# Issuing the mixer's streamed weights from SyncE's DMA queue instead of GpSimd's

## The chip, the core and the metric

The kernel runs on one core of a Trainium2 chip. The time is device microseconds of one execution; several executions give a median. All rows of a profile come from one profiled execution, which has a time of its own.

## What is computed

Four layers in a row on x of 2048 tokens by 640 numbers (bf16): attention with a recurrent memory (A), a mixer with an MLP (B), and both again with the same weights. Each layer is added to x after a layer norm.

```python
x = x + A(layernorm(x));  x = x + B(layernorm(x))
x = x + A(layernorm(x));  x = x + B(layernorm(x))

# A: 64 segments of 32 tokens, one after the other; 32 heads of 192
mem = mem0                                    # 8 x 640
for s in range(64):
    h = concat([mem, x[32*s:32*s+32]])        # 40 x 640
    q, k, v = h @ Wq, h @ Wk, h @ Wv          # 640 -> 32 x 192 each
    o = softmax(mask(q @ k.T * 192**-0.5)) @ v
    o = o @ Wo                                # 32 x 192 -> 640
    mem = o[:8];  out[s] = o[8:]

# B: c = 160, the four quarters of h moved by 1, -1, 2, -2 tokens
h  = gelu(layernorm(x) @ w1)                  # 640 -> 640
x1 = x + shift_quarters(h) @ w2               # 640 -> 640
y  = x1 + gelu(layernorm(x1) @ w3) @ w4       # 640 -> 1536 -> 640
```

## The kernel before

**Steps.** A segment needs the memory of the segment before it, so attention is a chain of 64 steps. The kernel runs both attention layers together: in step t, lane 0 is segment t of the first attention layer and lane 1 is segment t - 5 of the second (LAG = 5). There are 69 steps. The first five and the last five have one lane (40 columns in a matmul), the others two (80 columns). After each second step a chunk of the mixer (64 tokens of each lane, 128 rows) becomes ready; its work is spread among the matmuls of the steps that follow. There are 35 chunks.

**Weights.** Wq, Wk, Wv and Wo are cut into 8 groups of four heads. A group of Wq, Wk or Wv has five blocks of 128 rows by 768 columns (192 KB), a group of Wo has six of 128 by 640 (160 KB). They do not all fit in SBUF. By CUT, three blocks of each group of q, k and v and four of each group of o (two of the first) stay resident; the others are streamed from HBM anew in each step (block, lines 428 to 451, issued at line 447). The mixer's weights are streamed anew in each chunk: 5 blocks of w1, 5 of w2, 12 of w3 and 12 of w4, each 128 by 640 (load_b, lines 453 to 467, issued at line 465). The parts of w1, w3 and w2 that do not lie as a block in HBM are written once, at the start, in block order to a scratch tensor in HBM (wbd, order_mixer_weights, lines 469 to 490, from GpSimd's queue).

**The ring.** Streamed blocks of both kinds go into one ring of 16 slots (wst). Attention may hold at most 14 of them at a time (RING_A), the mixer at most 6 (RING_B). A slot comes free when TensorE has finished the matmuls on its block.

**The order.** Nothing is scheduled by the compiler. Every operation is added to a planner (Plan.add) with its engine, an estimated duration, a due time, and what it reads and writes. Plan.place (lines 134 to 246) plays the program through: at each turn it takes, of all engines, the operation that can start first, and among those of one engine that can start within 0.05 us (0.03 on TensorE) the one with the earliest due time. Streamed attention loads form the queue "wa" and mixer loads the queue "wb"; only the head of each is on offer. The order found is the order in which each engine's instructions are written; on the chip each engine runs its own list in that order and waits on semaphores.

Loads issued from SyncE (SP) obey one more rule: a load may start only when the tenth-last load of SP has landed, in the plan by est, and on the chip by a dependency that is written in at the end:

```python
def est(o, t):                                              # line 163
    s = max(t, o.ready)
    if o.dma and o.e == "SP" and len(landed) >= FLIGHT:     # FLIGHT = 10
        s = max(s, landed[-FLIGHT])
...
for o in placed:                                            # line 1094
    ins = o.fn(o)
    if o.dma and o.e == "SP":
        if len(flight) >= FLIGHT:
            tc.add_manual_dep(ins.ins, flight[-FLIGHT].ins.name, ...)
        flight.append(ins)
```

The mixer's loads are issued by one function, whose engine depends on a constant:

```python
def load_b(c, nm, n, due):                                  # line 453
    b = ring("rb")
...
    def fn(op):
        return (nc.sync if B_SP else nc.gpsimd).dma_start(out=T(b)[:, 0:Dm], in_=src)
    add("SP" if B_SP else "POOL", SP_US if B_SP else POOL_US, due, fn, r=rd, w=(b,),
        dma=P * Dm * 2, queue="wb")
```

**Other names.** TensorE's projections are at lines 530 (k and q) and 571 (v), the output projection at 669, scores, transposes and P V at 602, 635 and 650. The mixer's matmuls are at 939 (w1), 961 (w2), 993 (w3) and 1011 (w4). GpSimd also issues the loads and stores of activations (lines 823 to 834 and 1029) and computes the powers of the layer norms (741, 898).

Of the kernel before, what the change touches and what calls it, by code (L numbers as in the profile page):

```python
# [22 lines left out]
RING = 16  # L23
RING_A = 14
RING_B = 6
B_SP = False
POOL_US = 0.9
SP_US = 0.47
CUT = {"k": [3] * 8, "q": [3] * 8, "v": [3] * 8, "o": [2] + [4] * 7}
# [55 lines left out]
class Plan:  # L85
# [11 lines left out]
    def add(self, e, d, due, fn, r=(), w=(), a=(), dma=0, queue=None, after=()):  # L97
        op = Op()
        op.e, op.d, op.due, op.fn, op.dma = e, d, due, fn, dma
        op.succ, op.ready, op.n = [], 0.0, 0  # L100
        op.i = len(self.ops)
        preds = set(after)
        slots = []
        for b in r:
            preds.update(b.writers)
        for b in w:
            preds.update(b.writers)
            preds.update(b.readers)
        for b in a:
            preds.update(b.base)  # L110
            preds.update(b.readers)
        for b in r:
            b.readers.append(op)
        for b in w:
            b.base = [op]
            b.writers = [op]
            b.readers = []
        for b in a:
            b.writers.append(op)
        for b in {id(b): b for b in (*r, *w, *a)}.values():  # L120
            if isinstance(b, Slotted):
                b.left += 1
                slots.append(b)
        op.slots = slots
        preds.discard(op)
        for p in preds:
            p.succ.append(op)
            op.n += 1
        self.ops.append(op)
        if queue is not None:  # L130
            self.queues.setdefault(queue, []).append(op)
        return op
# [117 lines left out]
def kernel(  # L250
# [148 lines left out]
    def T(b):  # L399
        if b.obj is None:  # L400
            b.obj = b.make()
        return b.obj
# [50 lines left out]
    def load_b(c, nm, n, due):  # L453
# [10 lines left out]
        def fn(op):  # L464
            return (nc.sync if B_SP else nc.gpsimd).dma_start(out=T(b)[:, 0:Dm], in_=src)  # L465
        add("SP" if B_SP else "POOL", SP_US if B_SP else POOL_US, due, fn, r=rd, w=(b,), dma=P * Dm * 2, queue="wb")
        return b, lambda: T(b)[:, 0:Dm]
# [669 lines left out]
```

## Time and profile before

| | |
|---|---|
| median of 3 runs | 3576.57 us (3575.23 to 3577.35) |
| the profiled execution | 3575.23 us |
| its span, first to last instruction | 3573.5 us |
| mean granted TensorE clock | 0.989 |
| weight transfers from SP (line 447) | 4554, of 192 or 160 KB |
| weight transfers from GpSimd (line 465) | 1190, of 160 KB |
| bytes moved, mean rate | 1097.76 MB, 307 GB/s |

How to read it: PE is TensorE's matmuls and PEld its weight loads, DVE is VectorE, ACT ScalarE, POOL GpSimd, SP SyncE, and SPq the queue of instructions on SP, all of which issue or wait. A busy share is an average over the span. A row of waits names the engine and line that waited, after the arrow what ended the wait (an engine's instruction or a DMA's landing), and then the total in us, the number of times and the longest. "DMA share" is how much of the time the 16 DMA engines were moving packets, on average. Queue q1 carries what SP issues, q0 what POOL issues. A transfer of 128 rows is split among the 16 DMA engines; it has landed when all 16 are done.

### The profile page before, as it was taken

The page shows a single profiled execution, that of the slowest core. Times are in us where ns is not written, and L with a number is a line of the kernel's source. Part 1 is how long each engine was busy: PE and PEld are TensorE (multiplying, and loading weights), DVE is VectorE, ACT ScalarE, POOL GpSimd, SP SyncE. Part 2 cuts the span into 40 slices and gives each one's busy share as a digit, 9 for nine tenths or more (in the row PEclk, how much of TensorE's full clock was granted, in tenths as well). Part 3 has the DMA queues.
Part 4 walks back from the last instruction along what each step waited for, and adds up shares of the span by engine and source line. Part 5 has one row for each costly group of instructions (what it writes and reads, how often), then busy time and mean ns, then how long its engine had stood idle before and what let it go on. Part 6 is the DMA issues. An engine that isn't in the chain of part 4 may idle for free.

```text
span 3573.5 us, 194593 instructions
## 1 busy us (share of the span) xinstructions
PE 3398.9 (95%) x84703; PEld 3260.5 (91%) x84703; DVE 2384.2 (67%) x7085; ACT 1710.5 (48%) x3584; POOL 948.2 (27%) x1712
## 2 busy tenths in 40 slices
PE   5899999999999999999999999999999999999996
PEld 4788999999999999999999999999999999999885
DVE  2456667777676777776666777776767777776555
ACT  2344555554454555544455555454545555444432
POOL 3022222222222222222222222222222222222224
PEclk9999999999999999999999999999999999999898
DMA  9999999999999999999999999999999999999996
GB/s 342 310 314 312 305 302 304 310 308 308 309 307 313 314 308 304 316 300 308 306 308 311 311 301 305 308 319 308 309 311 310 311 306 313 309 304 316 310 313 207
DMA packets 735993, 1097.76 MB, mean 307 GB/s; under 512 B 97374, under 2 KB 693612, under 8 KB 735136
## 3 DMA queue, kind: packets, MB, share of 16 engines
q1 hardware_dynamic: 669504, 874.19, 74.6%
q0 software_dynamic: 65632, 211.12, 17.9%
q8 instruction: 662, 10.85, 1.3%
q14 instruction: 195, 1.60, 0.1%
HBM read 1079.68 MB, written 8.19 MB: 304 GB/s over the span
## 4 chain that ended last, share of the span: by engine, by line
PE 69%; DMA 19%; issue 9%; POOL 2%; DVE 1%; ACT 0%; POOLq 0%; SPq 0%; ACTq 0%; DVEq 0%
PE psy L669 14%; PE psq L530 12%; PE psv L571 11%; PE psk L530 11%; DMA wst<-in_A_Wk_dram 7%; DMA wst<-in_A_Wq_dram 5%; PE psvt L583 4%; DMA wst<-in_B_w_dram 4%; PE pss L602 3%; PE pso L650 3%; PE psh L993 3%; DMA wst<-in_A_Wv_dram 3%; PE pst L635 2%; PE y L1011 2%; POOL wst L465 1%
## 5 line engine op out<-in xcount | busy, mean ns | idle before, releaser
L530 PEld LDWEIGHTS <-wst 128*128 128x128 bf16 x13248 | 551.9, 100 | 75.1 <-DMA wst<-in_A_Wk_dram 41.3
L587 ACT COPY V<-psvt 80x768 bf16<-80x768 bf16 (+1 forms) x552 | 438.2, 794 | 327.7 <-PE psvt L583 326.2
L465 POOL DMA_DIRECT2D wst<-in_B_w_dram x560 | 303.6, 542 | 1005.2 <-PE psk L530 250.6
L656 DVE CAST oT<-pso 128x480 bf16<-128x480 f32 (+1 forms) x552 | 340.8, 617 | 341.7 <-PE pso L650 341.0
L465 POOL DMA_DIRECT2D wst<-wbd x630 | 339.6, 539 | 724.8 <-PE pss L602 229.5
L669 PE MATMUL psy<-oT,wo 128*128 128x80 bf16 (+1 forms) x10350 | 509.6, 199 | 11.2 <-DMA wo<-in_A_Wo_dram 5.1
L538 ACT CAST qT<-psq 128x480 bf16<-128x480 f32 (+1 forms) x552 | 292.3, 530 | 428.8 <-PE psq L530 427.5
L530 PE MATMUL psk<-hT,wk 128*128 128x80 bf16 (+1 forms) x9936 | 482.7, 199 | 7.9 <-ACT hT L707 4.2
L571 PE MATMUL psv<-hT,wv 128*128 128x80 bf16 (+1 forms) x9936 | 466.6, 199 | 6.5 <-DMA wv<-in_A_Wv_dram 4.3
L530 PE MATMUL psq<-hT,wq 128*128 128x80 bf16 (+1 forms) x9936 | 454.5, 199 | 9.8 <-DMA wq<-in_A_Wq_dram 8.7
L577 ACT CAST vTs<-psv 128x480 bf16<-128x480 f32 (+1 forms) x552 | 292.3, 529 | 337.2 <-PE psv L571 335.5
L669 PEld LDWEIGHTS <-wo 128*128 128x128 bf16 x10350 | 425.6, 100 | 21.3 <-issue 9.2
L530 PEld LDWEIGHTS <-wk 128*128 128x128 bf16 x9936 | 411.6, 99 | 21.9 <-issue 8.8
L571 PEld LDWEIGHTS <-wv 128*128 128x128 bf16 x9936 | 399.8, 100 | 18.7 <-DMA wv<-in_A_Wv_dram 5.7
L613 DVE CUSTOM_DVE_ANT_1 pss<-pss,mask 80x320 f32<-80x320 f32 (+1 forms) x512 | 245.4, 479 | 253.8 <-PE pss L602 252.3
L530 PEld LDWEIGHTS <-wq 128*128 128x128 bf16 x9936 | 395.5, 100 | 16.3 <-DMA wq<-in_A_Wq_dram 9.5
L530 PE MATMUL psk<-hT,wst 128*128 128x80 bf16 (+1 forms) x6624 | 359.0, 199 | 32.2 <-DMA wst<-in_A_Wk_dram 28.2
L571 PE MATMUL psv<-hT,wst 128*128 128x80 bf16 (+1 forms) x6624 | 368.0, 199 | 8.7 <-DMA wst<-in_A_Wv_dram 4.8
L625 DVE TENSOR_REDUCE sm<-pss 80x4 f32<-80x320 f32 (+1 forms) x552 | 252.7, 458 | 153.6 <-ACT pss L620 153.1
L669 PE MATMUL psy<-oT,wst 128*128 128x80 bf16 (+1 forms) x6210 | 353.0, 199 | 1.0 <-DMA wst<-in_A_Wo_dram 0.5
L530 PE MATMUL psq<-hT,wst 128*128 128x80 bf16 (+1 forms) x6624 | 333.2, 200 | 16.3 <-DMA wst<-in_A_Wq_dram 14.3
L546 DVE CAST kT<-psk 128x320 bf16<-128x320 f32 (+1 forms) x552 | 254.7, 461 | 136.9 <-PE psk L530 132.6
(119 smaller groups left out, 5768.8 us busy)
## 6 DMA issues: line engine op xcount, KB each, us to landing
wst<-in_A_Wk_dram SPq DMA_DIRECT2D x1104, 192.0 KB, 4.7
wst<-in_A_Wq_dram SPq DMA_DIRECT2D x1104, 192.0 KB, 4.9
wst<-in_A_Wv_dram SPq DMA_DIRECT2D x1104, 192.0 KB, 4.9
wst<-in_A_Wo_dram SPq DMA_DIRECT2D x1242, 160.0 KB, 4.4
wst<-wbd POOLq DMA_DIRECT2D x630, 160.0 KB, 5.1
wst<-in_B_w_dram POOLq DMA_DIRECT2D x560, 160.0 KB, 4.9
wk<-in_A_Wk_dram SPq DMA_DIRECT2D x8, 576.0 KB, 7.3
wq<-in_A_Wq_dram SPq DMA_DIRECT2D x8, 576.0 KB, 7.5
```

Source lines behind the costliest of these rows:

```text
L465: return (nc.sync if B_SP else nc.gpsimd).dma_start(out=T(b)[:, 0:Dm], in_=src)
L530: nc.tensor.matmul(out=o[:, c, 0:N], lhsT=w[:, c * P:(c + 1) * P], rhs=h[:, kc, c0:c0 + N], start=pq.begin(), stop=True, skip_group_check= ...
L538: nc.scalar.copy(out=q[:, :, 0:N], in_=T(pq)[:, :, 0:N])
L546: nc.vector.tensor_copy(out=k4[:, :, 0::3, 0:N], in_=p4[:, :, 0::2, 0:N])
L571: nc.tensor.matmul(out=o[:, c, 0:N], lhsT=w[:, c * P:(c + 1) * P], rhs=h[:, kc, c0:c0 + N], start=pv.begin(), stop=True, skip_group_check= ...
L577: nc.scalar.copy(out=vs[:, :, 0:N], in_=T(pv)[:, :, 0:N])
L583: nc.tensor.transpose(out=T(pt)[0:N, c, :], in_=vs[:, c, 0:N], identity=ident[:, :])
L587: nc.scalar.copy(out=V_[0:N, :, 0:Dh], in_=T(pt)[0:N].rearrange("n c f -> n (c f)").rearrange("n (i e) -> n i e", i=HG))
L613: nc.vector.tensor_tensor_reduce(out=o, in0=o, in1=maskt.unsqueeze(1).to_broadcast([N, HG, N]), scale=-scale, scalar=3.0e38, op0=ALU.add, ...
L625: nc.vector.reduce_sum(out=sm_[0:N, 4:4 + HG], in_=o, axis=AX.X)
L656: nc.vector.tensor_copy(out=o_[:, :, 0:N], in_=T(pso)[:, :, 0:N])
L669: nc.tensor.matmul(out=T(psy[j])[:, m - m0, c0:c0 + N], lhsT=w[:, m * P:(m + 1) * P], rhs=o_[:, c, 0:N], start=psy[j].begin(), stop=True, ...
```

## The change

One constant: the mixer's weight blocks are issued from SP, in the planner and on the chip. With it, the planner counts 0.47 us (SP_US) for each issue instead of 0.9 (POOL_US), both queues of weights share SP's list in one order, and the rule of ten transfers in flight holds for attention's and the mixer's loads together.

```diff
 RING = 16
 RING_A = 14
 RING_B = 6
-B_SP = False
+B_SP = True
 POOL_US = 0.9
 SP_US = 0.47
```

The ring, its limits, the sizes of the blocks, the resident weights and all arithmetic stay as they are. So do the other DMAs of GpSimd.

## The prediction

> **What bounds the kernel now.** I read the page first (busy times, DMA rows), then the table of stages, then who waits for whom on PE and SP, and last the issue and landing events of every weight transfer.
>
> ```profile
> PE 3398.9 (95%) x84703; PEld 3260.5 (91%) x84703; DVE 2384.2 (67%) x7085; ACT 1710.5 (48%) x3584; POOL 948.2 (27%) x1712
> ...
> q1 hardware_dynamic: 669504, 874.19, 74.6%
> q0 software_dynamic: 65632, 211.12, 17.9%
> ```
>
> Two things are near full: PE, and the 16 DMA engines (74.6 + 17.9, and 1.4 for instructions: 93.9%). POOL is at 27%. The table of stages tells which of the two leads where:
>
> ```profile
> 100.00:270.00 170.00, 154.75 (x4252) 137.20 (x4250) 88.71 (x333) 66.91 (x173) 30.13 (x55) 0.96 0.95 309
> 300.00:3200.00 2900.00, 2835.58 (x70439) 2763.82 (x70437) 2039.21 (x5883) 1460.83 (x2981) 762.10 (x1369) 1.00 0.94 308
> 3260.00:3500.00 240.00, 224.10 (x6034) 199.25 (x6033) 140.32 (x507) 99.42 (x249) 64.51 (x119) 0.94 0.95 314
> ```
>
> The columns are PE, PEld, DVE, ACT, POOL, then clock, DMA share and GB/s. In the long body (both lanes, 80 columns) matmuls of the projections start 36 ns apart; summing what each start-to-start interval exceeds its kind's median gives 4 to 5 us in each 100 us. So PE leads the body by a little and DMA follows at 94%. At both ends (one lane, 40 columns, median 25 ns) the same sum is about 26 us in 100: there DMA leads. The waits of PE in the body name transfers, attention and mixer alike:
>
> ```profile
> PE psk L530 <- DMA wst<-in_A_Wk_dram: 17.3, 31, 1.4
> PE y L1011 <- DMA wst<-in_B_w_dram: 13.3, 25, 1.5
> PE psq L530 <- DMA wst<-in_A_Wq_dram: 9.6, 14, 1.4
> ```
>
> For streamed k, q and v blocks in the body I paired each transfer with its first matmul: the block has landed 1.8 to 2.0 us before use in the median, and under 0.2 us before in 3% (v) to 10% (k) of cases. That is a thin cushion: a transfer that lands 1 us later is late one time in four or five.
>
> **A limit that the plan does not know.** FLIGHT = 10 is in both versions. In the trace every SP transfer signals one of eight semaphores, in strict turn (574 or 573 transfers on each), and SP waits on that semaphore before it issues the next transfer on it. So transfer k waits for the landing of k-8, and the ten can't be reached. POOL has eight others. SP's own waits show it:
>
> ```profile
> SPq L447 <- PE psy L669: 265.4, 404, 2.1
> SPq L447 <- PE psk L530: 227.5, 358, 2.4
> ...
> SPq L447 <- DMA wst<-in_A_Wk_dram: 60.8, 102, 1.4
> ...
> SPq L447 <- DMA wst<-in_A_Wq_dram: 45.4, 90, 2.3
> ```
>
> Those are of the body: 1632 us in all for PE to free a ring slot, 135 us for a landing. SP waits mostly for slots today, seldom for its eight.
>
> I count transfers between the end of their issue and their landing (one semaphore in eight has no landing record; I fill it with the median, 4.29 us). In the body the mean is 5.6 on SP and 1.8 on POOL, 7.4 together; more than eight are in flight for 27% of the time, more than twelve hardly ever. DMA delivers by that number: stretches of at least 3 us with 6 to 8 in flight (mean 6.9) moved 301 GB/s, 7 to 9 (8.0) 319, 8 to 10 (8.9) 335. The body needs 305, which is the count at 7.4. The same is seen early, where POOL's six blocks lie landed and unused until 161 us and SP works alone (6.0 in flight), and just after, with both (9.4):
>
> ```profile
> 113.00:168.00 55.00, 50.15 (x1441) 44.98 (x1437) 29.39 (x113) 22.79 (x59) 4.48 (x8) 0.97 0.93 289
> 168.00:215.00 47.00, 44.29 (x1172) 38.68 (x1170) 25.77 (x91) 19.16 (x47) 17.17 (x32) 0.97 1.00 339
> ```
>
> **The change, part by part.** It moves the 1190 mixer loads of load_b from POOL's queue to SP's; planner times and the rule of ten follow.
>
> 1. POOL loses 1190 issues of 0.54 us, 643 us. Worth nothing: at 27% it holds nobody but itself, and PE's waits that end in a LayerNorm step are some 2 us in the body. No cost if that cover goes, since it only gains time.
>
> 2. SP gains 1190 issues. Its shortest issue-to-issue pitch is 0.474 us, so 564 us more: 5776 issues need 2738 us, 77% of the span. SP's waits (some 2 ms) hide it; if they did not, the rate would be one transfer per 0.474 us against 0.62 needed, so SP's issue time alone is no bound. Queued behind a waiting mixer load are now all later attention loads, and PE waits for those; slots come free in PE's order, which the plan knows, so I add nothing for that, with rival C as the other end.
>
> 3. The eight semaphores now carry everything but 246 activation transfers of 80 KB or less. When SP is held by its eight today (48 runs of six or more issues after 100 us) it holds 6.9 in flight, not eight, because an issue ends 0.39 to 0.41 us after the landing that allowed it. So the ceiling is about 6.9, with POOL's remainder 7.0: 300 GB/s (301 at 6.9, 303 at 7.2 from windows of 20 us). Check from the other side: transfer k may go when k-8 has landed, seven issues after its own issue ended. SP's mean pitch in the body is 0.764 us today, seven are 5.35, less 4.29 for the landing: 1.06 us of margin. With the mixer's blocks the pitch is 3573.5 / 5776 = 0.62, seven are 4.33, and the margin is 0.04. From 270 to 3500 us the price is 3230 x (305/300 - 1) = **+54 us**. Its ends: 310 GB/s (7.7 in flight, if an even queue does better than one that swings between 5 and 11) gives 3230 x (305/310 - 1) = -52; 288 GB/s (6.4) gives +191. I take the middle since 6.9 is measured on this very queue.
>
> 4. The mixer's packets change from 5120 bytes (243 ns mean) to rows of 1280 (62.8 ns, the row of the o blocks on q1): per DMA engine 8 x 62.8 - 2 x 243 = 16 ns a transfer, x 1190 = **+19 us** of DMA time, on the path as far as DMA leads, which by step 3 it does. By medians (55 and 196 ns) it is 48 ns, 57 us; if PE leads, nothing.
>
> 5. The ring. POOL fetches mixer blocks whenever one of six slots is free. A mixer block lies landed for 11.3 us on average and holds its slot 16.7 us; mixers hold 5.6 of the 16 slots, attention lives on 9.4 with 7.3 us each. On one queue the planner picks the block due first, so mixer blocks should come later and attention's cushion grow: by Little's rule 16 slots over 1.61 transfers per us are 9.9 us for every block. What that is worth: at most the stalls of the body, 4.4% of 2900 = 130 us; at least nothing, since a cushion does not raise the rate of step 3. Where the ceiling binds I take only the early stretch: 55 us at 283 (weights alone) instead of 300 GB/s, **-3 us**.
>
> The Trainium skill, "DMA: Bandwidth & Descriptors", section "Issuing engines are not separate DMA queues", says that all issuing engines share the same 16 DMA engines, and a second issuer saves only issue time. By it step 3 would be nothing and the whole change the 564 us of issue time that SP's waits hide: 3575. The rows of 113 to 215 us speak against it as far as the second queue brings more transfers in flight.
>
> **The sum:** 54 + 19 - 3 = +70 on the profiled execution's own 3575.23 us (span 3573.5, 1.7 around it): 3645. That execution is 1.3 us under the median of the runs, 3576.57, which changes nothing here. 0.2% of it, 7 us, is about what a measurement of this kernel can tell from no change.
>
> **Rivals.**
> A, the forecast: the eight semaphores make DMA the bound. 3645, its own range 3590 to 3710. For it: the count by number in flight, and a margin that falls to nothing. Against: the counts mix cause with what was just queued. Chance 0.54.
> B, faster: freed slots let attention's blocks land well ahead, PE's stalls in the body halve: 3575 - 65 = 3510. For it: mixer blocks idle 11.3 us in the ring. Against: PE at that pace asks 311 GB/s, seven to eight in flight all the time. It decides if six to seven in flight, held evenly, move over 310. Chance 0.24.
> C, much slower: strict turn and one order. A landing out of turn or a mixer load without a slot holds SP, 6.4 in flight, 288 GB/s: 3575 + 191 + 19 = 3785. For it: 13% of SP's issues in the body already find the eighth-last transfer not landed. Against: SP alone held 6.9 where it was held by its semaphores. Chance 0.14.
> D, no difference: the smaller number in flight and the better use of slots cancel, or the eight are not what SP is held by after all; 3575. For it: DMA packets queue behind the same 16 engines anyway. Against: the margin of step 3. Chance 0.08, of it 0.06 within 0.2%, the rest slower.
>
> So faster 0.24, same 0.06, slower 0.70. The range leaves out the better part of C and the lower part of B: 3515 to 3760.
>
> **What would show it.** Step 3: SP's waits for landings rise from 135 us in the body to several hundred and those for PE fall; never more than eight in flight, mean near 6.9; DMA share at or above 0.94 with GB/s at 300 or less in every slice. Step 4: q0 almost empty, q1 at some 840 thousand packets (669,504 and 1190 x 144). Step 5: mixer blocks under 12 us in the ring, attention's over 8, and fewer waits of PE at L1011. If GB/s in the body is above 310, step 3 is wrong and B holds; if the waits of SP are for PE still, the slots and not the semaphores bind, and the forecast falls with them.

## The result, and the profile after

The changed kernel takes 3691.18 us in the median of 4 runs (3683.15 to 3704.55), beside 3576.96 for the kernel before (4 runs, one more than in the table above): a ratio of 1.0321, 95% interval 1.0282 to 1.036. Its profiled execution took 3704.55 us with a span of 3702.9. The forecast was 3645, range 3515 to 3760.

The page of the changed kernel, busy times and the two queues:

```profile
PE 3423.6 (92%) x84703; PEld 3281.4 (89%) x84703; DVE 2376.6 (64%) x7085; ACT 1712.3 (46%) x3584; POOL 306.2 (8%) x522
...
q1 hardware_dynamic: 840864, 1069.24, 89.9%
q0 software_dynamic: 8512, 16.08, 1.4%
```

The matmuls are the same in number, PE's share is three points lower: PE waits more. The 16 DMA engines, which now get nearly everything from one queue, are not fuller but a little emptier: 89.9 + 1.4 + 1.2 + 0.1 = 92.6% against 93.9%. So neither of the two that were near full before is full now. The table of stages of the changed kernel (PE, PEld, DVE, ACT, POOL, clock, DMA share, GB/s), with the two early stretches and the body:

```profile
113.00:168.00 55.00, 49.94 (x1397) 44.84 (x1393) 28.20 (x110) 22.49 (x57) 1.75 (x3) 0.94 0.92 292
168.00:215.00 47.00, 42.81 (x1133) 37.86 (x1131) 25.70 (x93) 19.39 (x48) 2.62 (x5) 0.92 0.94 297
300.00:3200.00 2900.00, 2744.60 (x67938) 2674.64 (x67938) 1963.67 (x5672) 1410.73 (x2881) 232.57 (x389) 0.99 0.93 298
```

Where before the early mixer loads lifted 289 GB/s to 339, there is no such rise now, and the body runs at 298 in place of 308. In the same 2900 us PE does 67938 matmuls in place of 70439, 3.6% fewer. Whom PE waits for in the body of the changed kernel:

```profile
PE y L1011 <- DMA wst<-in_B_w_dram: 53.9, 56, 2.8
PE psh L993 <- DMA wst<-wbd: 48.8, 31, 3.0
PE psq L530 <- ACT V L587: 20.4, 28, 0.7
PE psk L530 <- DMA wst<-in_A_Wk_dram: 11.7, 18, 3.2
```

The waits moved to the mixer's blocks: 103 us in the body (14 before), with 27 for attention's (29 before). That looks as if the mixer's blocks were fetched too late, a reading that had to be tested. SP's own waits in the body of the changed kernel, of 1286 us in all for PE to free a slot and 160 us for a landing:

```profile
SPq L447 <- PE psy L669: 161.6, 338, 2.4
SPq L447 <- PE psq L530: 129.7, 268, 1.9
...
SPq L447 <- DMA wst<-in_A_Wk_dram: 29.9, 71, 2.5
...
SPq L447 <- DMA wst<-in_A_Wq_dram: 29.4, 71, 1.8
```

More slots of the ring stand empty now. Counted from the start of a block's issue to the end of the last matmul on it, 12.8 of the 16 slots are held on average in the body (2.9 by the mixer, 9.9 by attention), in place of 15.4 before (5.6 and 9.8). The two issuers of before kept the ring nearly full; SP alone does not.

### The profile page after: what moved, and what is told of

Read it like the earlier page. It is cut to its first block, busy times and chain, and to the rows that moved or that the text cites. A ratio compares the mean times of both kernels' runs of the same rounds, so it can differ in the third digit from the quotient of the medians.

```text
span 3702.9 us, 194170 instructions
## 1 busy us (share of the span) xinstructions
PE 3423.6 (92%) x84703; PEld 3281.4 (89%) x84703; DVE 2376.6 (64%) x7085; ACT 1712.3 (46%) x3584; POOL 306.2 (8%) x522
## 3 DMA queue, kind: packets, MB, share of 16 engines
q1 hardware_dynamic: 840864, 1069.24, 89.9%
## 4 chain that ended last, share of the span: by engine, by line
PE 72%; DMA 24%; issue 2%; ACT 1%; SPq 0%; POOL 0%; DVE 0%; POOLq 0%; ACTq 0%; DVEq 0%
PE psy L669 14%; PE psk L530 13%; PE psq L530 12%; PE psv L571 12%; DMA wst<-in_B_w_dram 5%; DMA wst<-wbd 5%; PE psvt L583 4%; DMA wst<-in_A_Wq_dram 4%; PE pss L602 4%; DMA wst<-in_A_Wk_dram 4%; PE pso L650 3%; DMA wst<-in_A_Wv_dram 3%; PE psh L993 3%; PE y L1011 2%; PE pst L635 2%
## 5 line engine op out<-in xcount | busy, mean ns | idle before, releaser
L669 PE MATMUL psy<-oT,wo 128*128 128x80 bf16 (+1 forms) x10350 | 501.5, 200 | 8.8 <-DMA wo<-in_A_Wo_dram 5.3
L571 PE MATMUL psv<-hT,wv 128*128 128x80 bf16 (+1 forms) x9936 | 474.1, 200 | 3.3 <-DMA wv<-in_A_Wv_dram 2.7
L530 PE MATMUL psk<-hT,wk 128*128 128x80 bf16 (+1 forms) x9936 | 459.3, 199 | 2.7 <-DMA wk<-in_A_Wk_dram 1.4
L571 PEld LDWEIGHTS <-wv 128*128 128x128 bf16 x9936 | 407.5, 100 | 19.1 <-DMA wv<-in_A_Wv_dram 4.1
L530 PEld LDWEIGHTS <-wk 128*128 128x128 bf16 x9936 | 402.5, 100 | 16.9 <-DMA wk<-in_A_Wk_dram 2.4
L669 PE MATMUL psy<-oT,wst 128*128 128x80 bf16 (+1 forms) x6210 | 343.9, 200 | 8.8 <-DMA wst<-in_A_Wo_dram 8.5
L620 ACT ACTIVATE pss<-pss,sm 80x320 f32<-80x320 f32 (+1 forms) x552 | 261.7, 474 | 176.6 <-DVE sm L613 176.5
L640 ACT COPY PT<-pst 80x320 bf16<-80x320 bf16 (+1 forms) x552 | 221.8, 402 | 241.7 <-PE pst L635 232.2
```

What stands on the lines that cost most here:

```text
L530: nc.tensor.matmul(out=o[:, c, 0:N], lhsT=w[:, c * P:(c + 1) * P], rhs=h[:, kc, c0:c0 + N], start=pq.begin(), stop=True, skip_group_check= ...
L571: nc.tensor.matmul(out=o[:, c, 0:N], lhsT=w[:, c * P:(c + 1) * P], rhs=h[:, kc, c0:c0 + N], start=pv.begin(), stop=True, skip_group_check= ...
L620: nc.scalar.activation(out=o, in_=o, func=ACT.Exp, bias=sm_[0:N, 0:1], scale=-1.0)
L640: nc.scalar.copy(out=Pt[0:N, :, 0:N], in_=T(pst)[0:N, :, 0:N])
L669: nc.tensor.matmul(out=T(psy[j])[:, m - m0, c0:c0 + N], lhsT=w[:, m * P:(m + 1) * P], rhs=o_[:, c, 0:N], start=psy[j].begin(), stop=True, ...
```

## The experiments

Theory L: what counts is how many weight transfers are in flight; one issuer with eight semaphores holds fewer. Rival O: the planner's new order brings the mixer's blocks too late. Rival P: the smaller packets on one ring cost DMA time. Rival S: SP's serial pace, one issue per 0.474 us at best. All runs are read the same way, in the stage from 300 to 3200 us: transfers between the end of their issue and their landing (POOL's part includes its transfers of activations, 0.2 to 0.3), and GB/s of q0 and q1. What the theories and rivals lead to stands in each expectation.

| kernel | ratio to before (95%) | in flight SP + POOL | GB/s | PE's waits in the body for mixer / attention blocks, us |
|---|---|---|---|---|
| before | 1 | 5.6 + 1.8 = 7.4 | 305 | 14 / 29 |
| the change | 1.0321 (1.0282 to 1.036) | 6.4 + 0.3 = 6.6 | 294 | 103 / 27 |
| e1 | 1.0416 (1.0384 to 1.0447) | 6.3 + 0.3 = 6.6 | 293 | 22 / 111 |
| e2 | 0.9943 (0.992 to 0.9966) | 5.9 + 1.8 = 7.6 | 307 | 8 / 9 |
| e3 | 1.0529 (1.0498 to 1.056) | 5.0 + 1.5 = 6.5 | 289 | 42 / 92 |
| e4 | 1.0354 (1.0317 to 1.0391) | 6.4 + 0.3 = 6.6 | 295 | 26 / 94 |
| e6 | 1.0453 (1.0412 to 1.0494) | 5.2 + 1.7 = 6.8 | 291 | 11 / 124 |
| e7 | 1.1408 (1.1377 to 1.1439) | 5.1 + 0.2 = 5.3 | 266 | 167 / 127 |
| e8 | 0.9914 (0.9892 to 0.9937) | 5.1 + 2.5 = 7.6 | 307 | 9 / 1 |
| e9 | 1.0236 (1.0202 to 1.027) | 5.3 + 1.7 = 7.0 | 299 | 20 / 72 |
| e10 | 1.0467 (1.0421 to 1.0512) | 5.1 + 1.7 = 6.8 | 293 | 17 / 110 |

**e1: the old order, issued from SP.** The planner still books the mixer's loads on GpSimd, so every engine keeps the order of the kernel before; only the issuing engine differs.

```diff
-            return (nc.sync if B_SP else nc.gpsimd).dma_start(out=T(b)[:, 0:Dm], in_=src)
+            return nc.sync.dma_start(out=T(b)[:, 0:Dm], in_=src)
```

> Order of the kernel before on every engine, only the mixer's 1190 loads are issued from SP in place of GpSimd. Theory L (SP's eight semaphores hold down the number in flight): at most eight in flight, about 6.5 on average, some 293 GB/s, 3660 to 3720 us. Rival O (the new order fetches mixer blocks too late): the order is the old one, so 3570 to 3600 us, and PE's waits for mixer blocks stay near 17 us. Rival P (rows of 1280 bytes on one ring cost DMA time): about 3595 to 3640 us with DMA share near 0.95.

3723.79 us: a little over the range that L gave, and slower than the change itself. The order is the old one, so O cannot be the cause of this loss. The packets change with the issuer, so e1 says nothing against P. The body of e1, the stage's row and PE's waits:

```profile
300.00:3200.00 2900.00, 2753.62 (x67603) 2661.05 (x67599) 1950.52 (x5631) 1403.13 (x2863) 231.58 (x386) 1.00 0.93 296
```

```profile
PE psv L571 <- DMA wst<-in_A_Wv_dram: 50.1, 59, 2.5
PE psk L530 <- DMA wst<-in_A_Wk_dram: 34.0, 52, 2.3
PE y L1011 <- DMA wst<-in_B_w_dram: 21.5, 34, 1.8
```

Here attention's blocks come late and the mixer's mostly in time: 133 us together, against 130 in the change. The plan's order decides which blocks are late and hardly how long PE waits in all, though e1 as a whole is 33 us slower than the change.

**e2: the new order, issued from GpSimd.** The counterpart. B_SP = True for the planner, and load_b issues from GpSimd; the rule of ten stays with the attention loads, as it was.

```diff
-B_SP = False
+B_SP = True
...
-            return (nc.sync if B_SP else nc.gpsimd).dma_start(out=T(b)[:, 0:Dm], in_=src)
+            return nc.gpsimd.dma_start(out=T(b)[:, 0:Dm], in_=src)
...
-        if o.dma and o.e == "SP":
+        if o.dma and o.e == "SP" and o.i not in mixer:
```

> Order of the changed kernel on every engine, but the mixer's loads are issued from GpSimd, with its own eight semaphores. Theory L: more than eight in flight again, mean above 7, and with mixer blocks that hold the ring for 9 us in place of 17 it beats the kernel before: 3500 to 3570 us. Rival O: mixer blocks are still fetched late, PE's waits for them stay above 80 us, 3660 to 3700 us. Rival P: like the kernel before, 3560 to 3590 us.

3557.59 us: faster than both kernels. The body of e2, the stage's row and PE's longest waits for a transfer:

```profile
300.00:3200.00 2900.00, 2838.79 (x70972) 2777.95 (x70970) 2052.89 (x5936) 1473.59 (x3009) 783.22 (x1389) 1.00 0.95 311
```

```profile
PE psh L995 <- DMA wst<-wbd: 5.8, 7, 3.0
PE psk L532 <- DMA wst<-in_A_Wk_dram: 5.2, 6, 1.4
```

So the change has two halves of opposite sign. Its order is a gain: from before to e2, 0.57%; from e1 to the change, 3723.79 to 3691.18, 0.9%. Its queue is a loss: 4.2% with the old order (before to e1), 1.0321 / 0.9943 = 3.8% with the new.

**e3: at most eight together.** The kernel before, with the rule of ten made a rule of eight over SP's and GpSimd's weight transfers together.

```diff
-        if o.dma and o.e == "SP":
-            if len(flight) >= FLIGHT:
-                tc.add_manual_dep(ins.ins, flight[-FLIGHT].ins.name,
+        if o.dma and (o.e == "SP" or o.i in mixer):
+            if len(flight) >= CAP:                          # CAP = 8
+                tc.add_manual_dep(ins.ins, flight[-CAP].ins.name,
```

> The kernel before with one thing added: every weight transfer, of SP or GpSimd, waits for the landing of the eighth-last weight transfer in the order of the plan. Queues, packets and order stay. Theory L: the cap is what costs, so this alone gives 3640 to 3720 us, about 6.6 in flight and 295 GB/s. Rivals O and P: neither order nor packets change, 3575 to 3600 us.

3767.89 us, beyond the range. Order, queues and packets are those of before, so P is not needed for the loss. It overshoots; a likely reason is that this cap also ties the two queues together: SP waits 789 us in the body for landings, much of it for the mixer's. SP's waits in e3:

```profile
SPq L448 <- DMA wst<-wbd: 220.6, 250, 4.7
SPq L448 <- PE psy L672: 218.2, 410, 3.2
SPq L448 <- DMA wst<-in_B_w_dram: 154.0, 173, 3.6
```

**e4: the change, mixer loads due 8 us earlier.**

```diff
-        add("SP" if B_SP else "POOL", SP_US if B_SP else POOL_US, due, fn, ...
+        add("SP" if B_SP else "POOL", SP_US if B_SP else POOL_US, due - EARLY, fn, ...   # EARLY = 8.0
```

> The changed kernel with the mixer's loads due 8 us earlier than their matmuls in the planner, so that SP fetches them sooner. Theory L: the rate by the number in flight does not move; PE's waits for mixer blocks (115 us) go over to attention's blocks, 3670 to 3710 us. Rival O: PE's waits for mixer blocks vanish and nothing takes their place, 3580 to 3620 us.

3701.36 us, as L said. The mixer's blocks now lie landed for 7.7 us on average in place of 4.1, PE's waits for them fall from 103 to 26 us, and those for attention's rise from 27 to 94. Both times the sum is 120 to 130. Fetching the mixer's blocks earlier gains nothing, so O falls for the change too.

**e5: the kernel before with SP slowed, first try.** Four empty instructions ahead of each attention load.

> The kernel before with four empty instructions on SP ahead of every streamed attention load (4554 of them), so that SP is held up about as much in total as by the mixer's 1190 issues (some 500 us), while semaphores, queues and number allowed in flight stay. Rival S (SP's serial pace is the cost: in the changed kernel half of SP's issues follow at the shortest pitch of 0.474 us): 3640 to 3720 us. Theory L: SP's idle time takes it up, 3575 to 3610 us.

3574.98 us, ratio 0.9991 (0.9974 to 1.0009). The trace holds the same 4588 issues and 4594 semaphore waits on SP as before and nothing else: the empty instructions are not there. It is a repeat of the kernel before and tells nothing of S; it shows how well two runs of one kernel agree.

**e6 and e7: six in flight.** SP's rule of ten made a rule of six, in the kernel before (e6; GpSimd's loads stay free) and in the change (e7).

```diff
-            if len(flight) >= FLIGHT:
-                tc.add_manual_dep(ins.ins, flight[-FLIGHT].ins.name,
+            if len(flight) >= CAP:                          # CAP = 6
+                tc.add_manual_dep(ins.ins, flight[-CAP].ins.name,
```

> The kernel before, but SP may have six of its own transfers in flight, where its semaphores allow eight; GpSimd's stay free. Theory L: SP holds some 4.8 in place of 5.6, with GpSimd's 1.8 that is 6.6 together and about 295 GB/s: 3660 to 3740 us, without any change of order, packets or pace. Rivals S and P: SP had seldom more than six, 3575 to 3620 us.

> The changed kernel with six transfers of SP in flight in place of eight. Theory L, read off the rate by the number in flight (5.2 for 266 GB/s in place of 6.6 for 294): 3703 x 294 / 266, some 4050 to 4120 us. Rival S: the pace stays, 3700 to 3800 us. If it is steep, the changed kernel lies on the same curve as the kernel before.

e6: 3739.88 us, at the upper end of L's range; e7: 4082.79 us, in the range that L read off the rate by the number in flight. In e6 nothing but the number allowed changes, neither order nor packets, and SP issues no more than before. The stage's row and SP's waits for e6:

```profile
300.00:3200.00 2900.00, 2749.24 (x67403) 2658.28 (x67401) 1951.11 (x5623) 1403.77 (x2857) 734.54 (x1319) 1.00 0.92 295
```

```profile
SPq L448 <- DMA wst<-in_A_Wq_dram: 234.2, 353, 2.9
SPq L448 <- DMA wst<-in_A_Wk_dram: 223.5, 335, 2.9
```

**e8: e2, with 552 of o's blocks on GpSimd too.** The last block of each group of o is issued from GpSimd. In the trace those are 8 blocks in each of 69 steps, 552 transfers, and not the 621 of the expectation.

```diff
-                return nc.sync.dma_start(out=T(b)[:, 0:n], ...
+                return (nc.gpsimd if kind == "o" and c == GC - 1 else nc.sync).dma_start(out=T(b)[:, 0:n], ...
```

> e2, with the last of each group's streamed blocks of o (621 transfers) issued from GpSimd as well, to spread the transfers further over the two sets of eight semaphores. Theory L: SP is held less often, a little more in flight, 3530 to 3560 us against e2's 3558; where GpSimd's other waits hold up those blocks, PE waits at L669 and it is 3560 to 3600 us.

3547.25 us, 0.86% faster than the kernel before and the fastest of all. PE's waits for blocks in the body are 10 us. Its interval and e2's overlap a little (0.9892 to 0.9937, 0.992 to 0.9966).

**e9 and e10: the kernel before with SP slowed, second try.** One drain (e9) or two (e10) on SP ahead of each attention load.

> The empty instructions of e5 left no trace on SP (4588 issues and 4594 waits as before), so it tested nothing. Here one drain stands on SP ahead of each of the 4554 streamed attention loads; what it costs is read from SP's shortest pitch, 0.474 us before. Rival S (SP's serial pace): where the drains add some 0.1 us or more to an issue, as much as the mixer's issues add (564 us), 3640 to 3720 us. Theory L: up to a pitch of about 0.6 us within 1%, 3575 to 3615 us.

> The same with two drains ahead of each. Rival S: twice the loss of e9. Theory L: little, 3575 to 3630 us, as long as 4588 issues at the shortest pitch stay below three quarters of the span, as the changed kernel's are; beyond that SP itself becomes the bound.

The drains are there this time; a drain of e9, and an issue, with ns min/median/max after the count:

```profile
L449 SPq DRAIN  x4554: 115/128/146, 5.8 to 3596.7; - x198
```

```profile
L450 SPq DMA_DIRECT2D wst<-in_A_Wo_dram x1242: 327/328/1997, 24.9 to 3597.1; - x178
```

The body of e9, the stage's row and PE's longest wait:

```profile
300.00:3200.00 2900.00, 2790.09 (x69079) 2713.78 (x69077) 2000.68 (x5764) 1435.54 (x2928) 752.41 (x1352) 1.00 0.93 302
```

```profile
PE psk L533 <- DMA wst<-in_A_Wk_dram: 54.3, 60, 2.5
```

SP's usual pitch goes from 0.474 to 0.605 us in e9 and to 0.657 in e10. e9 took 3658.78 us, a ratio of 1.0236; e10 3739.15, 1.0467. That is what S said: e9 lies in its range, and e10 loses twice as much. It is not what L said (within 1% for e9). The number in flight fell too, from 7.4 to 7.0 and 6.8, though no limit on it was changed, and SP waits for landings even less than before (34 us in the body of e9): here the number in flight follows from the pace. 4588 issues at 0.605 us fill 2776 us of SP, about what the change's 5778 issues at 0.474 fill (2739). So SP's time is not free, though in the kernel before SP waits 1632 us of the body for slots: after a wait it often finds the next slots free as well, and can then only issue one load after the other. Of the kernel before 47% of SP's issues follow the one ahead within 5% of the shortest pitch, of the change 67%. Such an issue waits for nothing that a row of waits could show.

## Why the prediction was right, and where it was not

The direction held, and so did the link that rival A is built on: fewer transfers in flight, less moved per us, more time. That the loss comes from one queue in place of two (with the packets that go with it), and not from the order, is shown by e1 and e2. That the eight semaphores alone make it, as A has it, is not shown: SP's pace, which the forecast put at nothing, may do as much or more. The kernels of the table, with two orders, three ways of issuing, three with a cap and two with a slowed issuer, lie near one curve, from 5.3 in flight and 266 GB/s over 6.6 and 294 to 7.6 and 307; between 6.5 and 6.8 they scatter from 289 to 295. The curve by itself does not tell the cause, since a slower issuer has fewer in flight too. The loss was taken 44 us too small (70 forecast, 114 measured), and that it came so near is in part luck: by e1 the queue costs 149 us, where steps 2 to 4 had 73, and from e1 to the change the order gains 33, where step 5 had 3. The two misses cancel in part. The terms:

1. **POOL's relief:** worth nothing, as said. POOL went from 948 to 306 us busy.

2. **SP's issues:** this step failed: "SP's waits (some 2 ms) hide it". Its second reason, one transfer per 0.474 us against 0.62 needed, compares averages, and an issuer that first waits and then finds several slots free is not helped by its average. e9 adds about as much SP time as the change does (597 us against 564) and loses 2.4% without any change of queue or of the number allowed. That is more than half of the 4.2% of e1. It is a hint and no split: e9 spreads the time over attention's loads, while in the change it stands in the mixer's own issues.

3. **The eight semaphores:** the ceiling was about right, its use was not. Take runs of six or more issues after 100 us for which the landing of the eighth-last transfer came no earlier than 0.3 us before the issue ahead ended. The change has 168 of them (45 before); SP holds 6.9 in flight in them, as forecast, and q0 and q1 move 304 GB/s. But they fill only 879 us and are faster than the mean of 294 GB/s: I took the ceiling for the mean, and the loss lies between them, where SP waits for slots or climbs back at its own pace. The mean is 6.4, with POOL's rest 6.6. By the formula of the step, 3230 x (304.7 / 294.2 - 1) = 115 us, where it had +54.

   The signs that I had named are mixed. For the semaphores: 33% of SP's issues in the body find the eighth-last transfer not landed when the issue ahead ends, 13% before; it is 31% in e1, 20% in e2 and 4% in e9. Against them: SP's waits for landings rose only from 135 to 160 us in the body, not to several hundred, and e2, which is faster than the kernel before, has the same 160; the DMA share is 0.93 and not 0.94 or more; and GB/s is over 300 in 11 of the page's 40 slices. SP's waits for PE fell from 1632 to 1286 us but are still eight times those for landings. By the test that I had set myself ("if the waits of SP are for PE still, the slots and not the semaphores bind") the forecast should have fallen with them. It did not.

   I read it so (argued, not shown): the rows of waits leave out SP's pace, and a PE that is slowed by late blocks frees its slots later too. That 3.2 of the 16 slots stand empty on average speaks against a lack of slots as the bound, though a load waits for the one slot that the plan gave it. e6 shows that the number allowed costs by itself, e9 that the pace does. How the change's loss divides between these two is open; no run changed one of them in the changed kernel and left the other. (POOL's transfers beside the mixer's are 250 in the trace, 226 of them activations, and not 246; nothing rests on it.)

4. **The packets:** 19 us were on the sum. The rows of 1280 bytes took 64.2 ns on average (62.8 before), so a mixer transfer costs 8 x 64.2 - 2 x 243 = 28 ns more on each DMA engine, 33 us in all. But the engines are idle for 7.4% of the span instead of 6.1%, and for the same number in flight as much is moved: stretches of at least 3 us with 6 to 8 in flight move 302 GB/s in the body of either kernel, those with 4 to 6 move 267 before and 265 in the change. No sign of it in the time, but it was not tried by itself: the issuer and the packets always changed together. e3, e6 and e9 only show that losses of this size come about with the packets of before.

5. **The ring:** the size was wrong by far. A mixer block holds its slot for 8.9 us in place of 16.7, and mixers hold 2.9 slots in place of 5.6. I gave that 3 us, with the reason that a cushion does not raise the rate where the ceiling binds. The new order gained 33 us from e1 to the change, with the same queue; that it does so through the cushion is not shown. The 9.9 us for every block by Little's rule did not come: blocks of k, q and v hold their slots for 7.2 to 7.4 us, as before, since SP does not refill what the mixer frees, and PE's waits at L1011 rose from 13.3 to 53.9 us where they should have fallen. In e2, where GpSimd issues as well, 15.1 slots are held and blocks of k, q and v land 3.1 to 3.3 us before use (1.8 to 2.0 before).

The 149 us for the queue (e1: 4.16% of 3577) less 33 for the order make 116 beside the 114 measured, but that is no test of the split: both are differences to e1, which drops out. With the new order the queue costs 3.8% (e2 to the change), and on two queues the order gains 0.57%.

The Trainium skill, "DMA: Bandwidth & Descriptors", section "Issuing engines are not separate DMA queues", says that a second issuer saves only the time to issue, usually small beside the DMA. In this trace an issue from SP takes 0.474 us and a transfer 4.3 us to land, so it is small beside the DMA here as well. It is not without a price for that: e9, which adds 0.131 us to each of 4554 issues, loses 2.4%. And e1, which moves 1190 of 5744 loads to the other issuer with the order kept, costs 4.2%. Whether all of that is issue time, as the page's sentence has it, no run here shows; e6, which adds no issue time and allows fewer in flight, loses 4.5%. For the price of giving up the second issuer the measurement decides.

Of the rivals, B's mechanism shows in e2 and e8, where PE's waits for blocks fall from 43 us to 17 and 10, and was outweighed by the loss of the second queue; C's number of 6.4 was closer to the mean on SP than mine, without its reasons: in the body of the change no transfer of SP landed ahead of the one issued before it, and over the whole run SP waits for PE to free a slot 0.29 us per mixer load and 0.28 per attention load (341 us for 1190, 1265 for 4554), so a mixer load at the head holds it no longer than another.

## What to carry to other kernels

Count the transfers in flight and read the rate off that count, before and after a change of queues; the busy share of the DMA engines falls with the rate but by less (from 0.94 to 0.93 for 305 to 294 GB/s here). The count shows that the queue runs thin, not why: an issuer's pace and a limit on the number in flight both lower it. An issuer that waits half of its time may still be a bound, if it finds several slots free after a wait: look at the share of issues that follow at the shortest pitch. And test a change that does two things, here an order and a queue, one at a time: the half that is worth having may be hidden behind the other.

## What was not expected of the hardware

- With transfers of 160 and 192 KB, the rate rises from 5.3 in flight (266 GB/s) to 7.6 (307), by 15%, while the busy share of the DMA engines in the body rises from 0.86 to 0.95, by 10%.
- A drain on SP takes 0.128 us and lengthens the pitch by 0.131 us; a second one right after it adds only 0.052.
- Issued from SP, a 160 KB load goes in 128 packets of 1280 bytes at 55 ns in the median; issued from GpSimd it goes in 32 of 5120 at 196 ns, a tenth less per byte (by the means, 62.8 and 243 ns, 3% less). What that is worth in time was not tried by itself.
